# Gated linear attention before a ReLU-squared layer on one core: a chunk's first 32 keys join the state in one product, and every engine gets a written-out order

## The chip, the core and the metric

The kernel runs on one core of a Trainium2 chip. A core has a matrix engine (TensorE, PE in the profile; its weight loads are listed apart as PEld), three engines for elementwise work (VectorE or DVE, ScalarE or ACT, GpSimd or POOL), and a queue engine, SyncE or SP. SP, ACT and POOL also start DMA transfers. Each engine works through its own instructions in the order in which the program lists them, and waits on semaphores for the others. The metric is the device time of one execution in microseconds (us), the median of several runs; less is better. All inputs are float32.

## What is computed

For each of 4 x 8 (batch, head) pairs a complex decay runs over 768 steps of 48 features; its output feeds a two-layer block with a squared ReLU.

```python
mag = np.sqrt(a_re * a_re + a_im * a_im)
scale = np.minimum(mag, 0.999) / (mag + 1e-06)
a_re_n, a_im_n = (a_re * scale, a_im * scale)
for t in range(S):                       # S = 768, D = 48
    ar, ai = (a_re_n[:, :, t, :, None], a_im_n[:, :, t, :, None])
    new_re = ar * S_re - ai * S_im
    new_im = ar * S_im + ai * S_re
    kv = np.einsum('bhd,bhe->bhde', k[:, :, t], v[:, :, t])
    S_re, S_im = (new_re + kv, new_im)
    y[:, :, t] = np.einsum('bhd,bhde->bhe', q[:, :, t], S_re)
x = np.ascontiguousarray(y.transpose(0, 2, 1, 3)).reshape(B * S, H * D)   # 3072 x 384
h = x @ w_in                             # 384 x 2048
r = np.maximum(h, 0.0)
out = (r * r) @ w_out                    # 2048 x 384
```

## The kernel before

The 3072 rows are cut into 6 units of 512 steps (index `n`). In a unit the 8 heads form 4 pairs (index `i`, with `z = i // 2` for the half of the heads), and the 512 steps form 4 chunks of 128 (index `j`). For each unit the kernel works in these stages.

- `load` and `chain`: the inputs arrive in `aq` (gate, q, k) and `v`; DVE and ACT normalise the gates and multiply them up along the steps (a scan; its result is `xn`). `rest`/`apply` turn them into scaled queries and keys in `f`. Of the scaled keys, `gather` copies a version with the steps on the partitions into `KC`, by DMA.
- `turn` or `turn_pe`, once a pair: queries and keys are transposed into `QT`, with 96 rows (real and imaginary part of 48 features) and 128 columns for each chunk, head, and query or key. `turn_pe` does it on PE (line 1624) with ACT copies (line 1628), for the four pairs of unit 0 and three of unit 1; `turn` does it on DVE and with DMAs.
- `score(i, h)`, once a head: the 128 x 128 scores of each chunk, keys on the partitions of a PSUM bank (`sc`), steps on the columns (line 1645). A key acts only on later steps. So keys 0 to 63 are multiplied with all 128 steps and keys 64 to 127 with the last 64, in two products a chunk; each has 64 columns of weights, so one stands in PSUM partitions 0 to 63 and one in 64 to 127. In odd chunks the halves change places, so four successive products go to halves 0, 1, 1, 0. DVE then multiplies the bank with a mask (line 1648) into an `A` tile of 128 x 512.
- `keep(i)`: the state, 96 rows by 48 columns a head, grows by one chunk's keys times its `v` (line 1676, PSUM banks `tr`); sums go on DVE (line 1690), or on ACT where nothing came before (line 1686), into `St` and `S`.
- `mix(i)`: each chunk's output is `v` times the masked scores, 128 columns (line 1707), plus the state before the chunk times the queries, 128 columns (line 1711). The two heads of a pair write PSUM partitions 0 to 47 and 64 to 111. The state's product is left out where the sequence begins (chunk 0 of units 0 and 3, `fresh`) and where a new one begins inside a unit (chunk 2 of units 1 and 4, `cross`). ACT copies the result to `yt` (line 1720), a DMA brings it to `xT` (line 1733).
- `dense(n, grp)`: the first layer on `xT` (line 1758), squared ReLU on ACT (lines 1791 and 1792), then the second layer, as plain products (line 1806) or in `seven` by seven products of half size (line 1869) with sums on DVE (1885, 1894). `eleven` is the first layer of the last unit (line 2014). `rows` writes each 128 x 384 output tile with two DMAs on POOL's queue (line 1824).
- `convert` (lines 947 to 961): the weights arrive as raw 64-bit floats in tiles used for other things later (`KC`, `g`, `w`, `T`, `QT`, `xT`) and are turned into float32 by ACT and DVE; `fetch` (line 932) starts their DMAs on POOL's queue.

Nothing is issued at once. Every piece of work is a step with an engine, an estimated duration, keys that it reads and writes, and a rank; `Plan.order` runs them through a model of the engines' times, and `Plan.emit` issues them in the order of their modelled starts. Before, the engine takes the ready step of the lowest rank, and a table, `SHIFTS`, moves the ranks of some 200 steps by hand.

Of the kernel before, what the change touches and what calls it, by code (L numbers as in the profile page):

```python
# [16 lines left out]
ALU = mybir.AluOpType  # L17
# [464 lines left out]
class Plan:  # L482
# [3 lines left out]
    MARGIN = 0.3  # L486
    SLACK = 1.7
# [6 lines left out]
    SETTLED, GROUP = 90.0, 8  # L494
    HOLD, URGENT, FILL = {"DVE": 0.15, "ACT": 0.8}, (2, 0.2), (2, 0.2)
    DRAIN = {"DVE": 0.12, "ACT": 0.13}
    SHIFTS = {
        -1193.0: (320,),
        -802.0: (1256,),
        -595.0: (2284,),  # L500
        -594.0: (2285,),
        -500.0: (2041,),
        -301.0: (2694,),
        -210.0: (2688,),
        -108.0: (2690,),
        -100.0: (range(14, 17), 25, 37, 107, range(109, 111), 113, 166, 321, 344, 346, 356, 396,
            range(575, 577), 579, 625, range(1086, 1088), range(1245, 1247), 1271, 1304, 1306,
            1588, 1824, 1826, 2117, 2691, 2697, 2708, 2716,),
        100.0: (9, 11, range(20, 22), 24, 41, 104, 210, 234, 272, 279, 284, 304, 306, 314, 327,
            329, 331, 352, 354, 373, 375, 377, 379, 406, 408, range(410, 412), 417, 422, 424,  # L510
            range(431, 433), 440, range(443, 445), 448, range(452, 454), 466, 482, 496, 507, 564,
            range(681, 683), range(684, 686), 781, 783, 788, 800, 809, range(811, 814), 865, 869,
            885, 942, 1057, range(1116, 1118), 1123, 1129, 1132, 1146, 1164, range(1175, 1177),
            1188, range(1259, 1261), 1320, 1323, 1328, 1331, 1338, 1340, 1348, 1355, 1377, 1381,
            1384, 1389, 1392, 1406, 1478, 1480, 1729, 1737, 1740, 1748, 1763, 1781, 1792, 1794,
            range(1797, 1799), 1813, 1847, 1856, 1998, range(2043, 2045), 2071, 2073, 2135, 2147,
            2155, range(2163, 2165), 2180, range(2192, 2194), 2242, 2371, 2433,
            range(2445, 2447), range(2450, 2452), range(2456, 2458), 2459, 2472, 2474, 2545,
            2578, 2581, 2592, 2633,),
        189.0: (1283,),  # L520
        197.0: (2079,),
        200.0: (871,),
        292.0: (2097,),
        293.0: (2094,),
        302.0: (2233,),
        389.0: (2557,),
        503.0: (1815,),
        504.0: (1416,),
        588.0: (1405,),
        597.0: (1827,),  # L530
        602.0: (range(1665, 1668),),
        703.0: (1821,),
        793.0: (1345,),
        802.0: (2552,),
        805.0: (2616,),
        898.0: (779,),
        903.0: (378,),
        911.0: (441,),
        996.0: (2546,),
        1009.0: (1852,),  # L540
        1016.0: (831,),
        1209.0: (403, 425,),
        1516.0: (458,),
        1717.0: (484,),
        3014.0: (1380,),
        3126.0: (879,),
        3128.0: (419,),
        3315.0: (1166,),
        3422.0: (893,),
        3520.0: (1190,),  # L550
        4109.0: (27,),
        7784.0: (407,),
        9674.0: (414,),
        11185.0: (31,),
        11579.0: (35,),
        12886.0: (402,),
        12982.0: (39,),
# [30 lines left out]
    def order(self):  # L588
        steps = self.steps
        rank = [100.0 * s[4][0] + s[4][1] for s in steps]  # L590
        for shift, which in self.SHIFTS.items():
            for ns in which:
                for n in [ns] if isinstance(ns, int) else ns:
                    rank[n] += shift
        users = [[] for _ in steps]
        left = []
        for n, s in enumerate(steps):
            left.append(len(s[2]))
            for d in s[2]:
                users[d].append(n)  # L600
        engines = ("SP", "POOL", "PE", "DVE", "ACT")
        free = {e: 0.0 for e in engines}
        wait = {e: [] for e in engines}
        done, start, at = {}, {}, {}
        bus = warm = 0.0
        tiled = False

# [3 lines left out]
        def ready(n):  # L611
            e = steps[n][0]
            t = 0.0
            for d in steps[n][2]:
                same = steps[d][0] == e and steps[d][5] is None
                hop = self.HOP[steps[d][0]]
                if same:
                    hop = self.DRAIN.get(e, 0.0) if d in steps[n][7] else 0.0
                if e == "PE" and not same and done[d] > 100.0:
                    paired = steps[d][5] is not None and steps[n][6]  # L620
                    hop += self.SLACK if paired else self.MARGIN
                t = max(t, done[d] + hop)
            at[n] = t
            wait[e].append(n)

        for n in range(len(steps)):
            if not left[n]:
                ready(n)
        flown = {True: [], False: []}
        while len(start) < len(steps):  # L630
            best = None
            for e in engines:
# [66 lines left out]
def fast_path(ctx, tc, q, k, v, a_re, a_im, moe_w_in, moe_w_out, out, flag):  # L699
# [6 lines left out]
    C = 128  # L706
# [1470 lines left out]
```

## Time and profile before

| | us |
|---|---|
| median of 3 runs | 655.08 |
| the runs | 656.88, 655.08, 652.56 |
| the profiled execution, its time | 652.32 |
| the profiled execution, its span | 650.4 |

The profile is one execution. Its span runs from the first to the last instruction; the time of the same execution is 1.9 us more. Its granted TensorE clock was 0.991 of full speed in the mean. Line numbers such as L1645 are lines of the kernel before. A matmul of float32 stands in the trace as two records, each with its own weight load, so the 8 products of a score are 16 records. The profile gives for each engine its busy time, for each line its instructions, and for idle time what ended it. Neighbouring rows of the timeline overlap, because a product's record runs until its result is written; the pace is read from one start to the next.

### The profile page before, as it was taken

Reading aid. Unit: us, or ns where it says so; the run is one execution under the profiler, and the core shown is the slowest. Engines: PE = TensorE matmul, PEld = TensorE weight load, DVE = VectorE, ACT = ScalarE, POOL = GpSimd, SP = SyncE. Lnnn points to the kernel's source line nnn. Section 1 sums busy time; section 2 is a strip of 40 time slices with the busy share of each in tenths; the row PEclk is TensorE's granted clock in tenths of the full one; section 3 lists DMA queues with packets and bytes.
Section 4 is the critical chain, followed back from the end, with each engine's and each line's share of the span. In section 5 each row is a group of like instructions: output and inputs, shape, how many; then the busy total and the mean of one; then the engine's idle time right before and its main releaser. Section 6 shows DMA issues by size and latency. Waiting matters only on the chain.

```text
span 650.4 us, 12670 instructions
## 1 busy us (share of the span) xinstructions
PE 607.8 (93%) x4714; PEld 540.4 (83%) x4714; DVE 585.2 (90%) x1192; ACT 347.0 (53%) x635; POOL 122.0 (19%) x214
## 2 busy tenths in 40 slices
PE   0467999999999999999999999999999999999996
PEld 0356887688678988999989999989989989998996
DVE  7989999999998999998988999988998998459981
ACT  7479889888547244538353449354447442125500
POOL 7501140221100032040032030021040130051200
PEclk9979999999999999999999999999999999999999
DMA  6972787125620056452057580056370153377631
GB/s 210 298 268 50 162 220 202 42 50 147 174 53 1 1 126 163 127 156 41 7 144 176 128 182 2 13 138 177 101 183 0 26 132 92 82 240 270 213 116 30
DMA packets 55270, 80.39 MB, mean 124 GB/s; under 512 B 11392, under 2 KB 37920, under 8 KB 55200
## 3 DMA queue, kind: packets, MB, share of 16 engines
q0 software_dynamic: 15424, 42.12, 22.7%
q1 hardware_dynamic: 35168, 31.93, 19.3%
q10 hardware_dynamic: 4608, 5.44, 3.3%
q8 instruction: 39, 0.64, 0.4%
q14 instruction: 31, 0.25, 0.1%
HBM read 48.76 MB, written 4.72 MB: 82 GB/s over the span
## 4 chain that ended last, share of the span: by engine, by line
PE 72%; DVE 17%; DMA 5%; issue 2%; ACT 2%; POOL 0%; ACTq 0%; DVEq 0%; SPq 0%
PE d L1758 24%; PE d L1869 22%; PE d L1806 5%; PE sc L1645 4%; DVE f L1444 3%; PE yp L1707 3%; PE tr L1676 3%; PE yp L1711 2%; PE d L2014 2%; DMA w<-in_moe_w_in_dram 2%; PE tr L2014 2%; DVE g L1885 2%; DVE f L1509 2%; PE sc L2014 1%; DVE aq L1461 1%
## 5 line engine op out<-in xcount | busy, mean ns | idle before, releaser
L1758 PE MATMUL d<-xT,w 128*128 128x256 f32 x888 | 198.6, 380 | 1.5 <-DMA xT<-yt 1.2
L1758 PEld LDWEIGHTS d<-xT,w 128*128 128x128 f32 x888 | 167.3, 190 | 26.2 <-DMA xT<-yt 1.5
L1869 PE MATMUL d<-T,g 128*128 128x192 f32 x576 | 100.3, 329 | 0.3 <-DVE ot L1894 0.3
L1869 PEld LDWEIGHTS d<-T,g 128*128 128x128 f32 x576 | 93.6, 190 | 2.7 <-issue 1.1
L1791 ACT ACTIVATE g<-d 128x512 f32<-128x512 f32 x74 | 43.9, 593 | 69.9 <-PE d L1758 60.6
L1869 PE MATMUL d<-w,g 128*128 128x192 f32 x432 | 75.8, 328 | 0.0
L1869 PEld LDWEIGHTS d<-w,g 128*128 128x128 f32 x432 | 71.0, 190 | 1.2 <-ACT g L1791 0.2
L1824 POOL DMA_DIRECT2D out_dram<-ot x40 | 25.3, 638 | 218.4 <-DVE ot L1894 182.7
L1546 POOL DMA_DIRECT2D KC<-f x60 | 35.5, 600 | 112.2 <-DVE f L1509 82.6
L1885 DVE TENSOR_TENSOR g<-g 128x512 f32<-128x512 f32 x72 | 48.5, 684 | 7.6 <-ACT g L1792 4.4
L1792 ACT ACTIVATE g<-g 128x512 f32<-128x512 f32 x80 | 50.5, 631 | 2.5
L1444 DVE TENSOR_TENSOR f<-aq,xn 128x384 f32<-128x384 f32 (+1 forms) x72 | 46.8, 685 | 0.0
L1806 PE MATMUL d<-w,g 128*128 128x384 f32 x128 | 43.5, 489 | 0.2 <-DVE w L961 0.2
L1598 DVE STREAM_TRANSPOSE aq<-f 128x384 f32<-128x384 f32 (+1 forms) x51 | 42.2, 902 | 0.3
L1114 DVE TENSOR_TENSOR f<-aq 128x384 f32<-128x384 f32 x72 | 37.1, 552 | 0.5
L1645 PE MATMUL sc<-QT 96*64 96x64 f32 (+1 forms) x736 | 36.8, 249 | 0.5 <-ACT QT L1628 0.5
L1645 PEld LDWEIGHTS sc<-QT 96*64 96x64 f32 x736 | 34.2, 137 | 3.0 <-ACT QT L1628 1.2
L1806 PEld LDWEIGHTS d<-w,g 128*128 128x128 f32 x128 | 23.6, 190 | 15.4 <-DVE w L961 0.9
L1894 DVE TENSOR_TENSOR ot<-ot,d 128x192 f32<-128x192 f32 x70 | 23.3, 349 | 11.5 <-PE d L1869 11.2
L1475 ACT ACTIVATE f<-aq 128x768 f32<-128x768 f32 (+1 forms) x16 | 17.2, 1083 | 28.8 <-DVE aq L1461 28.7
L1037 POOL DMA_DIRECT2D v<-in_v_dram x30 | 23.2, 791 | 24.9 <-ACT f L1067 24.5
L1711 PE MATMUL yp<-QT,St 96*48 96x128 f32 x240 | 24.5, 272 | 0.0
(313 smaller groups left out, 1114.8 us busy)
## 6 DMA issues: line engine op xcount, KB each, us to landing
QT<-aq SPq DMA_DIRECT2D x136, 64.0 KB, 2.0
f<-in_moe_w_in_dram POOLq DMA_DIRECT2D x8, 768.0 KB, 8.1
f<-in_moe_w_out_dram POOLq DMA_DIRECT2D x8, 768.0 KB, 5.4
QT<-aq ACTq DMA_DIRECT2D x68, 64.0 KB, 2.3
KC<-f POOLq DMA_DIRECT2D x40, 96.0 KB, 3.4
out_dram<-ot POOLq DMA_DIRECT2D x40, 96.0 KB, 3.7
xT<-yt SPq DMA_DIRECT2D x34, 96.0 KB, 2.5
T<-in_moe_w_out_dram POOLq DMA_DIRECT2D x4, 768.0 KB, 11.0
```

The source lines that it names most:

```text
L1114: lambda c=c, j=j: dve.tensor_tensor(out=f[:, j], in0=a[:, :, :, c - 1], in1=a[:, j, :, c].unsqueeze(1).to_broadcast([C, 2, HH, D]), op=AL ...
L1444: lambda j=j, r=r: dve.tensor_tensor(out=f4[:, j, r], in0=a[:, r], in1=over(j), op=ALU.mult), rk)
L1546: lambda i=i, p0=p0, m=m, src=src, queue=queue: queue.dma_start(out=kc[p0:p0 + m, i], in_=src),
L1598: lambda src=src, dst=dst: dve.transpose(out=dst, in_=src), rank)
L1645: pe.matmul(sa[p0:p0 + CH, j, t0:], lhsT=T[:, j, 1, h, t0:t0 + CH], rhs=T[:, j, 0, h, t0:], start=True, stop=True)
L1711: pe.matmul(ps[64 * h:64 * h + D, j - js[0]], lhsT=at[j][:, h], rhs=T[:, j, 0, h], start=False, stop=True)
L1758: pe.matmul(ps, lhsT=w1[:, f // FP, m, ts(f % FP, C)], rhs=xT[:, n % 2, m, ts(grp, G)], start=(m == 0), stop=(m == NM - 1))
L1791: act.activation(out=o, in_=ps, func=AF.Relu)
L1792: act.activation(out=o, in_=o, func=AF.Square)
L1806: pe.matmul(ps, lhsT=gt[:, f % 2, ts(i, C)], rhs=w2[:, f], start=(f == 0), stop=(f == NF - 1))
L1869: pe.matmul(bank[b][:, 0:DH], lhsT=gsets[x][h][:, j - HW * h, r], rhs=w(j), start=first and j == 0, stop=last and j == NT - 1)
L1885: lambda: dve.tensor_tensor(out=g[:, :, o], in0=g[:, :, x0], in1=g[:, :, x1], op=op),
```

## The change

**The products.** A chunk's keys 0 to 31 act on its steps 0 to 31 in one block of 32 x 32 scores. Before, these scores are part of the `A` tile. Now DVE writes the masked block into rows 96 to 127 of the `QT` tile, below the 96 rows of the queries (`near`), and ACT copies `v`'s rows 0 to 31 into rows 96 to 127 of the state's tiles (`St`, `S`). One product of 128 rows then gives the state's part and this block's. The rest of the scores, steps 32 to 127, stays with `v` as a second product, of 96 columns. Both are now done for every chunk, so a state of zero is written by POOL where there was none. The rows under the queries of steps 32 to 127 must be zero: `clear` has POOL write them, again after the tiles have held raw weights.

A score now takes three products a chunk: keys 0 to 63 with steps 32 to 127 (96 columns, PSUM partitions 0 to 63); a 64-wide set of weights whose second half is keys 0 to 31, with steps 0 to 31 (32 columns, partitions 64 to 127); keys 64 to 127 with steps 64 to 127 (64 columns, partitions 64 to 127). The mask becomes two, for 384 columns and for 32 partitions by 128 columns.

**The layout.** In a chunk the steps are now grouped by 32 and not by 64, which needs four DMAs and not two for each output tile (`rows`). Odd chunks no longer change halves, so `v` and the gathered keys come in one DMA a chunk where odd chunks had two (`places`).

**The order.** `SHIFTS` and the choice by rank are gone. `ORDER` lists for each of the five engines the steps in the order in which it takes them (numbers count the engine's steps, sorted by rank). Steps of an engine start in that order and no other; the modelled times only interleave the engines.

```diff
-    SHIFTS = {
...
-        12982.0: (39,),
-    }
+    ORDER = {
+        "SP": """
...
+        "PE": """
+            539-554 0-1 555-559 2 560-561 3 562 4-7 563 8 564-567 42 568-571 45 572-573 43 574 44
...
+    }
     def places(i):
-        return [(CH, 0, CH), (0, CH, CH)] if i % 2 else [(0, 0, C)]
+        return [(0, 0, C)]
+
+    def clear(s, rank):
+        z = QT[s].rearrange("p (i h k x) -> p i h k x", i=W, h=2, k=2)[C - QC:C, :, :, 0]
+        keys = [("QT", s, 0), ("QT", s, 1)] + ([("t", 0), ("t", 1)] if s == 2 else [])
+        step("POOL", 0.9, [], keys, lambda: pool.memset(z, 0.0), rank)
...
             def go():
-                for j0 in range(0, W, 2):
-                    for half in range(2):
-                        for j in (j0, j0 + 1):
-                            p0, t0 = CH * (half ^ (j % 2)), CH * half
-                            pe.matmul(sa[p0:p0 + CH, j, t0:], lhsT=T[:, j, 1, h, t0:t0 + CH],
-                                      rhs=T[:, j, 0, h, t0:], start=True, stop=True)
+                for j in range(W):
+                    k0 = j * 4 * C + (2 * h + 1) * C
+                    for p0, at_, lo, hi in ((0, 0, QC, C), (CH, -QC, 0, QC), (CH, CH, CH, C)):
+                        pe.matmul(sa[p0:p0 + CH, j, lo:hi],
+                                  lhsT=QT[s][0:R, k0 + at_:k0 + at_ + CH],
+                                  rhs=T[:, j, 0, h, lo:hi], start=True, stop=True)
             step("PE", SCORE, [("QT", s, h)], [(b,)], go, rank, slack=True)
-            step("DVE", tt(L), [(b,)], AK[a], lambda: dve.tensor_tensor(
-                out=As[a].rearrange("p (j o t) -> p j o t", o=2, t=C),
-                in0=bank[b].rearrange("p (j o t) -> p j o t", o=2, t=C), in1=mask4,
-                op=ALU.mult), rank)
+            near = QT[s].rearrange("p (i h k t) -> p i k h t", i=W, k=2, h=2)[C - QC:C, :, 0, h, 0:QC]
+            step("DVE", tt(W * (C - QC)), [(b,)], AK[a], lambda: dve.tensor_tensor(
+                out=As[a][:, 0:W * (C - QC)].rearrange("p (j t) -> p j t", j=W),
+                in0=sa[:, :, QC:C], in1=far_mask, op=ALU.mult), rank)
+            step("DVE", tt(W * QC), [(b,)], [("q0", s, h)], lambda: dve.tensor_tensor(
+                out=near, in0=sa[C - QC:C, :, 0:QC], in1=near_mask, op=ALU.mult), rank)
...
+            step("ACT", ac(3 * 2 * D), [("v", vs(n))], [("sv", s)], lambda: act.copy(
+                out=sf[C - QC:C], in_=v5[0:QC, 1:W, 2 * i:2 * i + 2]), rank)
+            if cross:
+                step("POOL", 0.2, [], [("st", s, 2)], lambda: pool.memset(st[:, 1], 0.0), rank)
...
                         for h in range(2):
-                            pe.matmul(ps[64 * h:64 * h + D, j - js[0]], lhsT=v5[:, j, 2 * i + h],
-                                      rhs=aa[h][:, j], start=True, stop=at[j] is None)
+                            pe.matmul(ps[64 * h:64 * h + D, j - js[0]], lhsT=at[j][:, h],
+                                      rhs=T[:, j, 0, h], start=True, stop=False)
                         for h in range(2):
-                            if at[j] is not None:
-                                pe.matmul(ps[64 * h:64 * h + D, j - js[0]], lhsT=at[j][:, h],
-                                          rhs=T[:, j, 0, h], start=False, stop=True)
+                            pe.matmul(ps[64 * h:64 * h + D, j - js[0], QC:C],
+                                      lhsT=v5[:, j, 2 * i + h], rhs=aa[h][:, j],
+                                      start=False, stop=True)
...
+        if which[0] == 0:
+            Sn = Sb[n % 2]
+            if fresh:
+                step("POOL", 0.4, [], [("S", n % 2, i) for i in range(NP)],
+                     lambda: pool.memset(Sn[0:R], 0.0), (CHAIN, 0.3) if n == 0 else rank)
+            step("ACT", ac(DM), [("v", vs(n))], [("Sv", n % 2)], lambda: act.copy(
+                out=Sn[C - QC:C].rearrange("p (h d) -> p h d", h=H), in_=v5[0:QC, 0]), rank)
...
-        for p0 in (0, CH):
+        for p0 in range(0, C, QC):
             dma(pool, [("ot", o, 0), ("ot", o, 1)], [], lambda p0=p0: pool.dma_start(
-                out=out[r + p0:r + p0 + CH, :].rearrange("(t c) e -> c t e", c=W),
-                in_=ots[o][p0:p0 + CH]), (DENSE, n), CH * DM * 4)
+                out=out[r + p0:r + p0 + QC, :].rearrange("(t c) e -> c t e", c=W),
+                in_=ots[o][p0:p0 + QC]), (DENSE, n), QC * DM * 4)
```

In the rows below a name such as `sc_115` is a tile with its number, ahead of the arrow what is written, behind it what is read, then the shape that is written.

PE, unit 2 before: the end of a pair's two scores and what follows (L1645 is a score, L1869 the second layer, L1707 and L1711 the mix).

```order
L1645 MATMUL sc_115<-QT_75 64x128 x2
L1645 MATMUL sc_115<-QT_75 64x64 x2
L1645 MATMUL sc_115<-QT_75 64x128 x2
L1645 MATMUL sc_115<-QT_75 64x64 x2
L1645 MATMUL sc_116<-QT_75 64x128 x2
L1645 MATMUL sc_116<-QT_75 64x64 x2
L1645 MATMUL sc_116<-QT_75 64x128 x2
L1645 MATMUL sc_116<-QT_75 64x64 x2
L1869 MATMUL d_113<-w_67,g 128x192 x8
```

PE, unit 2 after: the end of a pair's scores, the first layer between, and the mix of the first chunks (L1674 is a score, L1805 the first layer, L1745 and L1748 the mix).

```order
L1674 MATMUL sc_116<-QT_74 64x96
L1674 MATMUL sc_116<-QT_74 64x32
L1674 MATMUL sc_116<-QT_74 64x64
L1805 MATMUL d_114<-xT,w_66 128x256 x3
L1805 MATMUL d_112<-xT,w_66 128x256 x6
L1805 MATMUL d_113<-xT,w_66 128x256 x6
L1745 MATMUL yp<-QT_74,S_88 48x128 x2
L1748 MATMUL yp<-xn,v_78 48x96
L1748 MATMUL yp<-e,v_78 48x96
L1745 MATMUL yp<-QT_74,St_92 48x128 x2
L1748 MATMUL yp<-xn,v_78 48x96
L1748 MATMUL yp<-e,v_78 48x96
```

A score goes from 8 products to 12, and every chunk's mix has four products, of 128, 128, 96 and 96 columns.

DVE before, the end of unit 0's attention: the masks of its last pair (L1648), state sums (L1690) and the conversion of weights around them (L954, L958, L961; L1070 is unit 1's chain).

```order
L954 TENSOR_SCALAR w_67<-w_67 128x768
L954 TENSOR_SCALAR w_67<-T 128x768
L961 ISA w_66<-xT,w_66 128x1536
L1648 TENSOR_TENSOR A_91<-sc_116,mask 128x512
L1070 TENSOR_TENSOR f_70<-f_70 128x768
L954 TENSOR_SCALAR w_66<-T 128x768
L1690 TENSOR_TENSOR St_93<-tr_118,St_93 96x96 x2
L961 ISA w_66<-T,w_66 128x1536
L954 TENSOR_SCALAR w_66<-g 128x768
L1648 TENSOR_TENSOR A_90<-sc_115,mask 128x512
L1648 TENSOR_TENSOR A_91<-sc_116,mask 128x512
```

DVE after, the same place (masks L1679 and L1682, state sums L1727, conversion L979, L983, L986).

```order
L1679 TENSOR_TENSOR A_91<-sc_116,mask 128x384
L983 SCALAR_TENSOR_TENSOR w_66<-g,w_66 128x768
L986 ISA w_66<-g,w_66 128x1536
L1727 TENSOR_TENSOR S_89<-tr_118,St_92 96x96
L986 ISA w_66<-w_67,w_66 128x1536 x2
L1679 TENSOR_TENSOR A_91<-sc_116,mask 128x384
L1682 TENSOR_TENSOR QT_75<-sc_116,mask 32x4x32
L1679 TENSOR_TENSOR A_90<-sc_115,mask 128x384
L1727 TENSOR_TENSOR St_93<-tr_118,St_93 96x96
L1682 TENSOR_TENSOR QT_75<-sc_115,mask 32x4x32
```

Other conversions than before stand ahead of the last masks, among them two of L958's kind (now L983) that came behind them.

POOL's queue at the start, before: the first transfers after the gates have arrived (L932 weights, L1021 q and k, L1037 v).

```order
L932 DMA KC_77<-in_moe_w_in_dram 128x3x512
L932 DMA g<-in_moe_w_in_dram 128x3x512
L1021 DMA aq_68<-in_q_dram 128x4x192
L1021 DMA aq_69<-in_q_dram 128x4x192
L1037 DMA v_78<-in_v_dram 64x8x48
L1037 DMA v_78<-in_v_dram 128x8x48
```

POOL's queue at the start, after (L957 weights, L1051 q and k).

```order
L957 DMA w_67<-in_moe_w_in_dram 128x3x512
L1051 DMA aq_68<-in_q_dram 128x4x192
L957 DMA w_67<-in_moe_w_in_dram 128x3x512
L1051 DMA aq_69<-in_k_dram 128x4x192
L1051 DMA aq_69<-in_q_dram 128x4x192
L957 DMA KC_77<-in_moe_w_in_dram 128x3x512
```

The weights for `KC_77`, first in the queue before, come seventh now, behind q and k and two other pieces of weights (k of `aq_68` stands ahead of these rows).

More of the change, by code (lines that the diff above doesn't have):

```diff
@@ L589, in order @@
         steps = self.steps
[L590 to L601, printed above, removed]
@@ L659, in order @@
+            sent = flown[e == "POOL"]
+            if steps[n][5] is not None and len(sent) >= self.LANES:
+                t = max(t, sent[-self.LANES] + self.LANDED)
+            return t
+        while len(start) < len(steps):
+            heads = [(ready(e), line[e][head[e]], e) for e in line if head[e] < len(line[e])]
+            t, n, e = min(h for h in heads if h[0] is not None)
+            head[e] += 1
             _, dur, _, _, _, wire, _, _ = steps[n]
@@ L804, in fast_path @@
     ypair = bank["yp"]
+    pool.memset(sums, 0.0)
     make_identity(nc, ident)
@@ L2085, in fast_path @@
         if n == 0:
+            for s in range(2):
+                clear(s, (CHAIN, 0.3))
+        if n == 0:
             for i in range(NPIECE):
```

318 lines of the change are left out of this document (175 added, 143 removed).

## Prediction

> **What bounds the kernel now.** I read the page first, then busy time by stage, the waits of PE, and PE's timeline.
>
> ```profile
> span 650.4 us, 12670 instructions
> ...
> PE 607.8 (93%) x4714; PEld 540.4 (83%) x4714; DVE 585.2 (90%) x1192; ACT 347.0 (53%) x635; POOL 122.0 (19%) x214
> ...
> PE 72%; DVE 17%; DMA 5%; issue 2%; ACT 2%; POOL 0%; ACTq 0%; DVEq 0%; SPq 0%
> ```
>
> PE and DVE are both nearly full, and the chain of work that ended last lies mostly on PE. A mean over the span doesn't say which one limits a stage, so I cut the span where PE's character changes. The columns are: stretch, length, busy time of PE, its weight loads, DVE, ACT, POOL, then granted clock and DMA.
>
> ```profile
> 0.00:20.00 20.00, 0.07 (x1) 0.08 (x1) 15.86 (x25) 14.65 (x27) 13.83 (x46) 1.00 0.75 219
> 20.00:42.50 22.50, 12.49 (x65) 11.74 (x65) 20.59 (x63) 12.32 (x26) 7.29 (x10) 0.77 1.02 342
> 42.50:84.40 41.90, 35.18 (x474) 28.80 (x474) 41.59 (x92) 36.82 (x68) 4.36 (x8) 1.00 0.44 104
> 84.40:640.00 555.60, 554.66 (x4144) 494.69 (x4145) 505.50 (x1010) 283.19 (x515) 96.53 (x151) 1.00 0.43 114
> 640.00:650.40 10.40, 5.39 (x34) 5.10 (x32) 1.69 (x5) 0.00 (x0) 0.00 (x0) 0.93 0.13 36
> ```
>
> There are two regimes. From 42.5 to 84.4 us DVE is busy 41.59 of 41.90 us: unit 0's attention hangs on DVE, and PE waits. From 84.4 to 640 us PE is busy 554.66 of 555.60 us, and DVE has 50 us to spare. From about 90 us on, PE's waits for others are these:
>
> ```profile
> PE d L1869 <- DVE ot L1894: 0.3, 1, 0.3
> PE tr L1676 <- DVE S L1690: 0.2, 1, 0.2
> PE d L1806 <- DVE w L961: 0.2, 1, 0.2
> ```
>
> So no order of steps can win anything there: the end is the moment at which PE becomes full, plus PE's work from then on, plus the tail. A change is worth what it adds to PE's work in units 1 to 5, and what it does to the 84.4 us.
>
> Busy time could hide idle time here, since records overlap. So I take the pace from starts, in unit 2 (start, length, engine, line, tiles and shapes, records).
>
> ```profile
> 240.92 4.15 PE L1758 MATMUL d<-xT,w 128*128 128x256 f32 x18
> 245.01 1.56 PE L1645 MATMUL sc<-QT 96*64 96x128 f32 x32
> 246.49 2.86 PE L1758 MATMUL d<-xT,w 128*128 128x256 f32 x12
> ...
> 255.27 0.84 PE L1676 MATMUL tr<-v,KC 128*64 128x48 f32 x23
> 255.89 0.32 PE L1645 MATMUL sc<-QT 96*64 96x128 f32 x1
> 255.94 0.22 PE L1676 MATMUL tr<-v,KC 128*64 128x48 f32 x1
> 256.00 1.52 PE L1645 MATMUL sc<-QT 96*64 96x128 f32 x31
> ...
> 264.15 0.43 PE L1707 MATMUL yp<-A,v 128*48 128x128 f32 x4
> 264.40 0.39 PE L1711 MATMUL yp<-QT,S 96*48 96x128 f32 x4
> 264.62 0.39 PE L1707 MATMUL yp<-A,v 128*48 128x128 f32 x4
> ...
> 265.94 0.26 PE L1676 MATMUL tr<-v,KC 128*64 128x48 f32 x4
> ```
>
> The first layer's 18 records of 256 columns take 4.09 us, 0.227 each, with no hole. In the mix four records of 128 columns (two heads, two records each) start every 0.22 us. The heads write different halves of the partitions and run side by side, so one half does a 128-column record in 0.11 us. A pair's two scores occupy PE from 245.01 to 246.49, 1.48 us.
>
> **The scores.** Before, each half of the array gets, for two chunks, two records of 128 columns and two of 64: 2 x 0.11 + 2 x 0.056 = 0.33 us. Two scores are four times that, 1.33, and 0.15 for starting and draining: the 1.48 measured. After, a chunk gives the lower half two records of 96 columns (0.165 us by the same rate) and the upper half two of 32 and two of 64. Counted in columns this is balanced, 96 and 96, and a score would cost what it did. But each of those records loads 64 columns of weights. What does a record cost whose weights are wider than its moving side? The state's products show it: 64 columns of weights, 48 moving. Twelve such records on one half (24 in all, the other half's have 33 columns) take from 255.27 to 256.00, 0.061 each with the first one's start, and not the 0.041 of 48 columns. A second place shows it more strongly, at a halved clock, in filling products with 128 columns of weights:
>
> ```profile
> 36.55 0.59 PE L1564 MATMUL d<-yt,ident 128*128 128x24 f32 x2 [8.49 <-DVE yt L1201]
> 36.97 4.60 PE L1564 MATMUL d<-ident 128*128 128x128 f32 x20
> 41.38 0.52 PE L1148 MATMUL tr<-ident,xn 128*128 128x128 f32 x3
> ```
>
> Two records with 24 moving columns take 0.42 us, 0.21 each; twenty with 128 take 4.41, 0.22 each. The narrow ones gain nothing. So a record of 32 columns behind 64 columns of weights should cost what one of 64 does, 0.057. The upper half then needs 4 x 0.057 = 0.228 us a chunk, and sets the pace; two scores take 8 x 0.228 + 0.15 = 1.97 us. That is 0.49 more a pair. Units 1 to 5 have 20 pairs: **+9.7 us**. The bounds: no more than the columns (0.165 a chunk), +0; or each start waiting for the one ahead of it in program order, which I price below at +13.4. I stay near 9.7 because the state's products are the nearest row.
>
> **The mix.** Before, a chunk with a state takes 2 x 0.22, a pair 1.76 us (264.15 to 265.94 is 1.79). After it takes 0.22 + 0.165 a chunk, 1.54 a pair. But the pairs of units 1, 3 and 4 skipped one chunk's state product, 7 x 0.22 = 1.54, and now do it. Only the 8 pairs of units 2 and 5 gain: **-1.8 us**. In units 0, 1, 3 and 4, two thirds of the pairs, the joint product gains nothing.
>
> **The start.** Until 84.4 us DVE decides, so I count its rows from the first use of `xn` to unit 0's last mask.
>
> ```profile
> L1648 DVE TENSOR_TENSOR A<-sc,mask 128x512 f32<-128x512 f32 x28 | 18.3, 681 | 1.9 <-PE sc L1645 1.9
> L1690 DVE TENSOR_TENSOR St<-tr,St 96x96 f32<-96x96 f32 x32 | 7.7, 248 | 0.9 <-PE yp L1711 0.4
> ...
> L954 DVE TENSOR_SCALAR w<-T 128x768 uint32<-128x768 uint32 x5 | 2.8, 553 | 0.0
> ...
> L961 DVE CUSTOM_DVE_ANT_0 w<-g,w 128x1536 uint16<-128x1536 uint16 x2 | 1.9, 962 | 0.1
> L958 DVE SCALAR_TENSOR_TENSOR w<-g,w 128x768 uint32<-128x768 uint32 x2 | 1.9, 953 | 0.0
> ```
>
> ```profile
> L1509 DVE TENSOR_TENSOR f<-f,aq 128x384 f32<-128x384 f32 x20 | 10.5, 550 | 0.1
> ```
>
> Ahead of the last mask stood 6 conversions of L954's kind and 3 of L961's, 6 x 0.55 + 3 x 0.96 = 6.2 us. Now it is 5, 4, and 2 of L958's kind: 2.75 + 3.84 + 1.91 = 8.5. Each of the 8 masks becomes one over 384 columns (0.55, as L1509) and one over 32 partitions, which no row shows: I take the state sum's 0.25 (96 x 96), between nothing and that; together 0.12 more than 0.68, in all +1.0. One state sum fewer: -0.25. The sum is +3.0, or about +2.5 by starts, since neighbouring records overlap by 0.08. Against it stand two idle times of DVE in the scan, and the row of the first full work of PE:
>
> ```profile
> 34.11 0.43 DVE L1197 TENSOR_TENSOR KC<-yt 128x96 f32<-128x96 f32 x2 [0.83 <-ACT yt L1222]
> ...
> 35.89 0.30 DVE L1197 TENSOR_TENSOR KC<-yt 128x36 f32<-128x36 f32 x2 [0.34 <-ACT yt L1222]
> ```
>
> ```profile
> 80.06 1.28 DVE L1648 TENSOR_TENSOR A<-sc,mask 128x512 f32<-128x512 f32 x2
> ```
>
> ```profile
> 84.38 1.53 PE L1758 MATMUL d<-xT,w 128*128 128x256 f32 x6 [1.25 <-DMA xT<-yt]
> ```
>
> ACT's copies of L1222 came behind weight conversions; in the new order they stand ahead of them, so 1.2 us can go. The last masks (80.06) release the last mix, its copy, its DMA, and PE's first layer at 84.38. I take 2.5 - 1.2 = **+1.3 us**, with -2 to +4 as its range. Unit 0's eight longer scores lie under DVE's work.
>
> **What I cost at nothing.** On DVE 40 masks of 0.12 more, 5 us, under the 50 idle us of the full stretch. On ACT 30 copies of `v`, 0.25 to 0.5 each, some 10 us, where 283 of 555 are used. POOL gets 40 more output issues and 15 memsets, and loses 24 gather and `v` issues; SP loses 12.
>
> ```profile
> L1824 POOL DMA_DIRECT2D out_dram<-ot x40 | 25.3, 638 | 218.4 <-DVE ot L1894 182.7 <-ACT ot L1811 25.2 <-DVE f L1114 7.6
> ```
>
> An output tile now needs four issues of 0.64 us, so its buffer comes free 1.3 us later, and DVE's sums into the next one are queued behind that wait; POOL waits 218 us at this line, so there is room. If these covers fail, the price is a PE wait of a microsecond or two at a unit's seam. At the start the conversion of the `KC` weights stands in ACT's queue ahead of the scan's copies:
>
> ```profile
> 27.77 0.48 ACT L1163 COPY e<-tr 128x384 f32<-128x384 f32 x1
> ```
>
> ```profile
> KC<-in_moe_w_in_dram POOLq DMA_DIRECT2D x1, 768.0 KB, 5.0
> ```
>
> That transfer landed 5.0 us after its issue when it was first. Now 3.1 MB go ahead of it; at the 342 GB/s of the second stretch that is 9 us more, about 23 us on the clock. The scan's copies run at 27.8, so some 4 us cover it.
>
> **The sum.** 652.3 + 9.7 - 1.8 + 1.3 = 661.5 us for the profiled execution. That execution lies 2.8 us under the median of 655.1, so I add the same 9.2 to the median: **664 us**, 1.4% slower. About 1%, 6.5 us, is what a measurement of this kernel can tell from no change.
>
> **The rivals.**
>
> *Weight loads hide, not slower.* If a 32-column record costs its 32 columns, 0.028 us, half against half stays balanced and the scores cost nothing: 655.1 - 1.8 + 1.3 = 655. The place is the upper half in L1674; there are 40 scores x 8 such records. The change turns from within 1% to slower when the record costs more than about 0.05 us (320 records x 0.022 = 7). For it speaks that the two halves load their weights apart; against it speak the 24-column rows. Chance 0.12.
>
> *Starts in program order.* If no product may start ahead of one that precedes it, a chunk costs 0.08 (the second 96-column start) + 3 x 0.057 = 0.25 us, a score 1.0 against 0.67, and 40 scores +13.4: 668. The rows at 255.89 and 255.94 speak against it: a score's record starts before the last record of the state's products, which precede it in the program. Chance 0.08. The Trainium skill, "TensorE: Matmul & The Clock Gate", Part 3, The mechanism, states this rule (strict FIFO for starts, no reordering); the trace disagrees at those two rows.
>
> *New waits.* The order has no choice at run time: one late transfer (the `KC` weights, `v` behind the weights, the zeroed rows on POOL) holds an engine and all behind it. At 5 us or more it gives 669 to 675. Against it: the 4 us of cover. Chance 0.07.
>
> *The order wins at the start.* Slower scores and all, faster by over 1% needs some 16 us out of the first 84; DVE's idle time there is 8.5 us, mostly before the gates arrive. Chance 0.06, with 640 to 648.
>
> **How the numbers follow.** My forecast has 0.67. About a fifth of it stays under 6.5 us (0.14, same), the rest is slower (0.53). With the second and third rival slower is 0.66; same is 0.14 and 0.11 from the first rival, 0.25; faster is 0.06 and small parts of the rest, 0.09. The range, 654 to 672, leaves out the fourth rival, half of the first, and the worst of the third: 2 in 10.
>
> **What would show it.** Two scores between other work should take 1.9 to 2.0 us from start to start where 1.48 stood; 1.5 would refute the largest term. The mix of a pair in units 2 and 5 should take 1.54. PE should stay full after its first long run of first-layer work, and that run should begin at 84 to 88 us. A PE wait of several microseconds after 90 us would show a cover that failed; PE's first long run before 80 us would prove me wrong about the order.

## The result, and the profile after

The changed kernel took 663.89 us (median of 4 executions, 663.46 to 665.14) where the kernel before took 654.99: a ratio of 1.0141, with a 95% interval of 1.0105 to 1.0177. 664 was predicted. In the experiments below 14 of 64 executions (those with 32 columns of weights apart) took 8 to 11 us longer than the others of their kernel; the medians leave these out, and so do the ratios, except that of the run without the near product, which holds two.

The page of the changed kernel, its span, busy times and the chain that ended last:

```profile
span 662.1 us, 13619 instructions
...
PE 617.8 (93%) x5162; PEld 550.5 (83%) x5162; DVE 594.5 (90%) x1240; ACT 359.0 (54%) x665; POOL 139.8 (21%) x243
...
PE 84%; DVE 10%; ACT 2%; DMA 2%; issue 1%; ACTq 0%; DVEq 0%; SPq 0%
```

Busy time by stage (the same columns as before), and all waits of PE for others between 88 and 655 us:

```profile
42.50:84.40 41.90, 37.27 (x530) 30.69 (x530) 40.86 (x92) 38.79 (x72) 5.76 (x9) 0.96 0.37 89
84.40:651.50 567.10, 565.42 (x4560) 506.20 (x4560) 515.62 (x1058) 299.13 (x550) 112.96 (x181) 1.00 0.42 112
651.50:662.10 10.60, 3.24 (x20) 2.95 (x19) 1.24 (x4) 0.00 (x0) 0.00 (x0) 0.76 0.15 45
```

```profile
PE d L1916 <- DVE g L1932: 0.7, 1, 0.7
PE d L1805 <- ACT g L1838: 0.5, 1, 0.5
PE sc L1674 <- issue: 0.3, 1, 0.3
```

The picture is that of before, made longer: PE is full from 84 us on, DVE has some 51 us to spare there, and no wait over 0.7 us stands on PE. In PE's timeline, at a place in unit 2, stand the mix of a pair and behind it two scores:

```profile
256.25 0.43 PE L1745 MATMUL yp<-QT,S 128*48 128x128 f32 x4
...
257.82 2.04 PE L1674 MATMUL sc<-QT 96*64 96x96 f32 x48
259.79 4.17 PE L1916 MATMUL d<-w,g 128*128 128x192 f32 x24
```

The scores take from 257.82 to 259.79, 1.97 us, where 1.48 stood; that is the predicted number. The mix takes 1.57, from 256.25 to 257.82 (1.79 before, 1.54 predicted).

For the whole kernel I gave each record of PE the time from its start to the next record's start, with idle holes apart, and added up by kind of step from the end of unit 0's last mix. "Start" is the moment at which that mix ended, less 0.217 us for each record of the first layer that PE had done by then (2 before, 6 after), and those records are counted with the first layer. "Before again" is a second profiled execution of the kernel before. The last two columns are experiments that leave out part of the work: the near product, which is that of a chunk's keys 0 to 31 with its steps 0 to 31, and most of the mask that follows it.

| us | before | before again | after | no near product | and small near mask |
|---|---|---|---|---|---|
| start | 83.9 | 84.9 | 86.3 | 85.8 | 85.6 |
| scores | 29.7 | 29.7 | 38.1 | 27.9 | 27.7 |
| state products | 14.9 | 14.9 | 15.7 | 16.3 | 16.4 |
| mixes | 34.0 | 34.0 | 31.7 | 33.2 | 32.5 |
| first layer | 209.7 | 210.2 | 209.0 | 209.3 | 209.2 |
| second layer and the rest | 272.3 | 272.2 | 272.5 | 273.7 | 273.2 |
| PE idle | 0.9 | 1.7 | 1.5 | 4.3 | 2.2 |
| tail behind PE's last product | 5.0 | 5.5 | 7.4 | 5.6 | 5.5 |
| span | 650.4 | 652.9 | 662.1 | 656.1 | 652.4 |

From "before again" to "after" that is 8.4 for the scores, 0.9 for the state products (which partly run beside the scores), -2.3 for the mixes, +1.4 at the start, -1.2 in the first layer and +1.9 in the tail, 9.2 us with the small rows, as the spans give (652.9 and 662.1). The first profile's execution was 2.5 us shorter, so against it the span rose by 11.7. The tail was not in my sum. Its rows, before and then after (PE's last products, DVE's last sums into the output tiles, the output transfers):

```profile
642.63 2.76 PE L1869 MATMUL d<-T,aq 128*128 128x192 f32 x16
642.83 0.35 DVE L1894 TENSOR_TENSOR ot<-ot,d 128x192 f32<-128x192 f32 x1 [1.59 <-PE d L1869]
643.21 0.33 SPq L1818 DMA_DIRECT2D out_dram<-ot  x1
645.43 0.35 DVE L1894 TENSOR_TENSOR ot<-ot,d 128x192 f32<-128x192 f32 x1 [2.25 <-PE d L1869]
645.82 0.38 ACTq L1818 DMA_DIRECT2D out_dram<-ot  x1
```

```profile
653.28 1.46 PE L1916 MATMUL d<-T,aq 128*128 128x192 f32 x8
654.78 1.27 DVE L1941 TENSOR_TENSOR ot<-ot,d 128x192 f32<-128x192 f32 x4 [6.14 <-PE d L1916]
655.16 2.09 SPq L1865 DMA_DIRECT2D out_dram<-ot  x3
656.09 0.41 ACTq L1865 DMA_DIRECT2D out_dram<-ot  x1
```

Before, one sum and one transfer were left when PE ended. After, four sums wait 6.14 us for PE and then four transfers go out. PE's last steps stand in another order: the product that the first of the four sums needs comes last, and the other three queue behind it on DVE.

### The profile page after: what moved, and what is told of

The parts are those of the page before. It is cut to its first block, busy times and chain, and to the rows that moved or that the text cites. A ratio compares the mean times of both kernels' runs of the same rounds, so it can differ in the third digit from the quotient of the medians.

```text
span 662.1 us, 13619 instructions
## 1 busy us (share of the span) xinstructions
PE 617.8 (93%) x5162; PEld 550.5 (83%) x5162; DVE 594.5 (90%) x1240; ACT 359.0 (54%) x665; POOL 139.8 (21%) x243
## 4 chain that ended last, share of the span: by engine, by line
PE 84%; DVE 10%; ACT 2%; DMA 2%; issue 1%; ACTq 0%; DVEq 0%; SPq 0%
PE d L1916 27%; PE d L1805 27%; PE d L1853 6%; PE sc L1674 6%; PE yp L1745 3%; PE tr L1713 2%; PE yp L1748 2%; PE d L2061 2%; PE tr L2061 2%; PE sc L1805 2%; PE sc L2061 1%; DVE f L1474 1%; PE tr L1654 1%; PE yp L2061 1%; PE yp L1805 1%
## 5 line engine op out<-in xcount | busy, mean ns | idle before, releaser
L1805 PE MATMUL d<-xT,w 128*128 128x256 f32 x888 | 198.1, 380 | 0.5 <-ACT g L1838 0.5
L1805 PEld LDWEIGHTS d<-xT,w 128*128 128x128 f32 x888 | 167.5, 190 | 25.1 <-ACT g L1838 0.9
L1871 POOL DMA_DIRECT2D out_dram<-ot x80 | 48.3, 608 | 137.5 <-DVE ot L1941 115.7
L1576 POOL DMA_DIRECT2D KC<-f x48 | 31.0, 652 | 201.1 <-DVE f L1539 93.3
L1674 PE MATMUL sc<-QT 96*64 96x96 f32 (+2 forms) x1104 | 49.3, 235 | 0.3 <-issue 0.3
L1674 PEld LDWEIGHTS sc<-QT 96*64 96x64 f32 x1104 | 46.2, 137 | 2.5 <-issue 2.1
L1628 DVE STREAM_TRANSPOSE aq<-f 128x384 f32<-128x384 f32 (+1 forms) x51 | 43.6, 908 | 0.3
L1941 DVE TENSOR_TENSOR ot<-ot,d 128x192 f32<-128x192 f32 x70 | 23.4, 348 | 14.9 <-PE d L1916 14.5
L1745 PE MATMUL yp<-QT,St 128*48 128x128 f32 x268 | 27.0, 273 | 0.0
L1759 ACT COPY yt<-yp 112x512 f32<-112x512 f32 (+1 forms) x20 | 11.6, 578 | 26.2 <-PE yp L1748 24.8
```

Of the source, the lines that this page charges most:

```text
L1628: lambda src=src, dst=dst: dve.transpose(out=dst, in_=src), rank)
L1674: pe.matmul(sa[p0:p0 + CH, j, lo:hi], lhsT=QT[s][0:R, k0 + at_:k0 + at_ + CH], rhs=T[:, j, 0, h, lo:hi], start=True, stop=True)
L1745: pe.matmul(ps[64 * h:64 * h + D, j - js[0]], lhsT=at[j][:, h], rhs=T[:, j, 0, h], start=True, stop=False)
L1805: pe.matmul(ps, lhsT=w1[:, f // FP, m, ts(f % FP, C)], rhs=xT[:, n % 2, m, ts(grp, G)], start=(m == 0), stop=(m == NM - 1))
L1871: dma(pool, [("ot", o, 0), ("ot", o, 1)], [], lambda p0=p0: pool.dma_start(out=out[r + p0:r + p0 + QC, :].rearrange("(t c) e -> c t e", c= ...
```

## The experiments

**The kernel before, once more.** No edit.

> The kernel before, run and profiled once more, to see where its executions differ. The profiled one took 652.3 us, 2.7 under the median of the runs. If the difference is in the tail (from the start of the last product's end at 645.4 to the end of the span, 5.0 us there), the 7.7 us tail of the changed kernel is partly chance; I expect the tail within 0.5 us of 5.0, and the 2 to 4 us more of a usual execution ahead of 84 us, in the transfers and in PE's clock there.

654.89 us, span 652.9. Start +0.9 against the first profile, idle +0.8, tail 5.5, first layer +0.5; the scores and mixes are the same to 0.1. So executions differ by a microsecond at the start and by half a one in the tail, and the 7.4 of the changed kernel is outside that.

**Narrower weights: 32 columns.**

```diff
-for p0, at_, lo, hi in ((0, 0, QC, C), (CH, -QC, 0, QC), (CH, CH, CH, C)):
-    pe.matmul(sa[p0:p0 + CH, j, lo:hi], lhsT=QT[s][0:R, k0 + at_:k0 + at_ + CH],
+for p0, m, at_, lo, hi in ((0, CH, 0, QC, C), (C - QC, QC, 0, 0, QC), (CH, CH, CH, CH, C)):
+    pe.matmul(sa[p0:p0 + m, j, lo:hi], lhsT=QT[s][0:R, k0 + at_:k0 + at_ + m],
```

> The product of a chunk's first 32 keys loads 32 columns of weights (the 32 keys alone, written to the last 32 partitions) where it loaded 64. Theory (a record costs the wider of its two sides): the upper half then needs 2 x 0.028 + 2 x 0.057 = 0.17 us a chunk, about the lower half's 0.165, two scores take 1.5 us where 1.97 stood, 20 pairs give 9.4 us back: 654.5 us (653 to 657). Rival, a fixed price of 0.057 for any short record: two scores stay at 1.97, 664. Rival, starts in program order: 0.194 a chunk, 1.70 for two scores, 658.5.

719.8 us for the profiled execution (six lie between 719.8 and 745.4), ratio on record 1.1111 (1.1063 to 1.1158): worse than every theory. Two scores, between a mix and the second layer:

```profile
276.12 4.23 PE L1675 MATMUL sc<-QT 96*64 96x96 f32 x48
280.28 0.92 PE L1917 MATMUL d<-w,g 128*128 128x192 f32 x4
```

4.16 us, 0.52 a chunk. The records of 32 columns of weights carry the tile 96*32 in the trace, those around them 96*64, and the array changes tile size twice a chunk. The Trainium skill, "TensorEngine Tiling (Array Packing)", Key Properties, says that a change of the tiling mode drains the array. The trace agrees so far: (4.16 - 1.97) / 8 = 0.27 us a chunk for two changes. The run said nothing on what weights cost, since it changed a second thing that I had not thought of.

**Wider moving side.** `(CH, -QC, 0, QC)` becomes `(CH, -QC, 0, CH)`.

> The same product with 64 moving columns (steps 0 to 63) behind its 64 columns of weights where it had 32; the 32 added columns lie where the mask is zero or the third product writes over them. Theory (the wider side counts): free, two scores stay at 1.97 us and the time at 664 (663 to 666). Rival, a record costs its moving columns and something fixed on top: 16 records of a score pair's upper half with 32 more columns, 16 x 0.027 = 0.43 us a pair, 672.5 us.

664.7 us, ratio 1.0145 (1.0123 to 1.0168). Two scores:

```profile
258.05 2.04 PE L1674 MATMUL sc<-QT 96*64 96x96 f32 x48
260.02 0.59 PE L1916 MATMUL d<-w,g 128*128 128x192 f32 x2
```

1.97 again. Twice the moving columns behind the same weights are free, so the columns are not what the near product costs.

**The tail's order.** In PE's list `530-531 533-535 537-538 536 532` becomes `530-538`.

> PE's last eight steps (the halves of the last output tiles' second layer) stand in the order in which they stood in the kernel before; all else is that of the changed kernel. In the changed kernel four sums of DVE and four output transfers come behind PE's last product, before one sum and one transfer. Theory: the tail from PE's last product to the end of the span goes from 7.7 us back to about 5.0 to 5.6, and the time to 661.5 (661 to 662.5). Rival: a transfer's own time sets the tail, and it stays within 0.5 us of 7.7, 664.

662.4 us, ratio 1.0118 (1.0101 to 1.0135). Its profile, with a span of 670.6 us, holds the event that the last section shows; its tail is as before the change:

```profile
661.94 2.76 PE L1916 MATMUL d<-T,aq 128*128 128x192 f32 x16
...
664.74 0.35 DVE L1941 TENSOR_TENSOR ot<-ot,d 128x192 f32<-128x192 f32 x1 [2.25 <-PE d L1916]
665.12 0.38 ACTq L1865 DMA_DIRECT2D out_dram<-ot  x1
```

One sum and one transfer at the end, 5.9 us behind PE where 7.4 stood, and 1.5 us of the time, the smaller end of what I expected.

**Narrower weights without a change of tile: 33 columns.**

```diff
-for p0, at_, lo, hi in ((0, 0, QC, C), (CH, -QC, 0, QC), (CH, CH, CH, C)):
+for p0, m, at_, lo, hi in ((0, CH, 0, QC, C), (CH, QC + 1, 0, 0, QC), (CH, CH, CH, CH, C)):
...
-in0=sa[C - QC:C, :, 0:QC], in1=near_mask
+in0=sa[CH:CH + QC, :, 0:QC], in1=near_mask
```

> As the run with 32 columns of weights, but with 33 (32 keys and the one behind them), so that the product keeps a tile of 64 columns, as the state's products with 33 columns do; it is written to partitions 64 to 96, and the near mask reads partitions 64 to 95 there and writes to 96 to 127 as ever. Theory (a record costs the wider of its sides, and what the 32-column tile cost was the change between tile sizes, (4.16 - 1.97) / 8 = 0.27 us a chunk): no change of tile size, upper half 2 x 0.03 + 2 x 0.058 = 0.176 us a chunk, two scores 1.5 to 1.6 us where 1.97 stood; 20 pairs give 8 to 9.4 us back, and up to 2 more in unit 0, where PE is full from 70 us on: 653.5 us (652.5 to 656). Rival, a fixed price of 0.058 for any short record: 1.97 for two scores, 664. Rival, any change of weights' width within a half drains it: about 4.1 for two scores, 720.

663.0 us, ratio 1.0128 (1.0099 to 1.0156). And together with the tail's order:

> The 33 columns of weights and the last eight steps of PE in the order of the kernel before, both together. If the two are independent, 1.5 us less than with the 33 columns alone: 652 us by the theory, 662.5 by the rival of a fixed price per record.

659.7 us, ratio 1.0082 (1.0052 to 1.0113). That is 3.3 us below the 33 columns alone, where 1.5 was expected; in the two profiles the tail is 8.2 and 6.0 us, which shows 2.2 of it, and the rest is open. In the second run two scores take

```profile
551.02 1.81 PE L1675 MATMUL sc<-QT 96*64 96x96 f32 x48
552.77 0.43 PE L1917 MATMUL d<-w,g 128*128 128x192 f32 x1
```

1.75 us: neither my 1.5 to 1.6 nor the rival's 1.97. Weights' width counts, but half as much as I had said. The records' own starts on the upper half, from 551.24 us on, suggest the reason: within a chunk they are 28, 33, 86 and 58 ns apart, the sum 0.205 us. In the changed kernel's profile, with 64 columns of weights throughout, the same four are 31, 58, 86 and 58, the sum 0.233, which is four times 58. A stream of 64 columns takes about 55 ns, by the lower half's records of 96 columns, which start every 82. So the mended rule is that a load is hidden behind the *preceding* record's stream: one step costs the greater of this record's moving columns and the next record's weight columns. After the second short stream a load of 58 sticks out. The rule is read from the sums; the single starts don't show it step by step (33 and 86 stand where it has 58 and 58).

**The order within a score.** The near products of the four chunks stand together:

```diff
+for j, part in ((0, 0), (0, 1), (1, 1), (2, 1), (1, 0), (3, 1),
+                (0, 2), (2, 0), (1, 2), (2, 2), (3, 0), (3, 2)):   # part 0: lower, 1: near, 2: upper
```

> The run with 33 columns of weights and the old tail, and the 12 products of a score in another order: the four near products stand together, then the upper half's four others. With 33 columns two scores took 1.74 us, not the 1.5 to 1.6 that I had expected; the starts on the upper half are 28, 33, 86, 58 ns apart, 0.205 us a chunk. Theory, mended: a record's stream hides the next record's weight load, so that the step from one record to the next costs the greater of the one's moving columns and the other's weight columns. After a near record (28 ns of stream) a load of 64 columns (58 ns) sticks out, once a chunk, which gives 28 + 58 + 58 + 58 = 0.202. Grouped, it sticks out once a score: 7 x 28 + 9 x 58 = 0.718 us a score, 1.44 + 0.15 = 1.59 us for two, 3 us less over 20 pairs: 657 us (656 to 658). Rival, a load of 33 columns has a price of its own of 44 ns wherever it stands: 8 x 44 + 8 x 58 = 0.816 a score, 1.74 for two as before, 660.

> The same order of products, but with 64 columns of weights for the near product, as in the changed kernel (old tail too). Every load takes 58 ns and no stream is longer, so by the mended theory the order changes nothing: 16 x 58 = 0.93 us a score, 1.97 for two, 662.4 us, the time of the run with the old tail alone. If the grouping itself wins (less of the start and drain, or a better fit of the two halves), this run shows it: 1.8 or less, 659.

With 33 columns 659.0 us, ratio 1.0062 (1.004 to 1.0083); with 64 columns 662.2, ratio 1.0107 (1.0073 to 1.0142). First 33 (in a profile with a span of 668.1 that holds the last section's event, ahead of these rows), then 64:

```profile
561.36 1.67 PE L1676 MATMUL sc<-QT 96*64 96x96 f32 x48
562.96 0.43 PE L1918 MATMUL d<-w,g 128*128 128x192 f32 x1
```

```profile
258.43 2.04 PE L1676 MATMUL sc<-QT 96*64 96x96 f32 x48
260.40 0.43 PE L1918 MATMUL d<-w,g 128*128 128x192 f32 x1
```

1.60 against 1.59 expected, and 1.97 against 1.97: the mended rule holds, and a price of its own for each narrow load does not. That 1.59 came so close is partly luck. On the upper half the second score starts 0.752 us after the first, not 0.718: the narrow records follow each other every 33 ns, not 28, so there the load of 33 columns sets the step (7 x 33 + 9 x 58 = 753). What two scores take beyond that is 0.10 us, not 0.15. The time fell by 0.7 us (1.3 by the ratios, whose intervals overlap), not by the 3 that 20 pairs give. Something gives the rest back.

**What gives it back.** The near product is dropped from the changed kernel's list, with the old tail: `((0, 0, QC, C), (CH, CH, CH, C))`.

> The changed kernel with the old tail, the product of a chunk's first 32 keys and steps left out (its mask still runs, on what stands in the bank). The lower half's two records of 96 columns then set the pace, 0.165 us a chunk: two scores take 1.48 us, and the time falls by the whole price of that product, 20 x 0.49 = 9.8 us by the prediction, 662.4 - 9.8 = 652.6 us. Unit 0's scores, if they count too, would take off up to 2 us more: 650.6.

657.8 us, where 652.6 was expected (ratio 1.008, 1.0044 to 1.0116). By the table the scores fell by 10.2 us, as they should. But PE's idle time rose by 2.8, its mixes by 1.5, the second layer and the rest by 1.2. PE's waits from 88 us on:

```profile
PE d L1916 <- DVE g L1932: 1.4, 1, 1.4
PE yp L1745 <- DVE QT L1682: 0.8, 3, 0.3
PE d L1805 <- ACT g L1838: 0.6, 1, 0.6
PE tr L1654 <- ACT T L1658: 0.4, 1, 0.4
PE yp L1748 <- DVE xn L1679: 0.3, 1, 0.3
PE sc L1674 <- issue: 0.2, 1, 0.2
```

The mix (L1745, L1748) now waits for both masks (L1682 near, L1679 far). To see whether the masks are the cause, the near mask was cut to a quarter, `near[:, 0:1]` for `near`, once with the near product and once without:

> The changed kernel with the old tail, and the near mask of each score made over one chunk's row instead of four (32 x 32 elements for 32 x 128: the rest is left out). DVE saves some 0.1 us 48 times, 5 us. Theory: with scores at 1.97 us DVE keeps its cover, so PE is not served sooner, and the time stays at 662.4 (661.5 to 663). Rival: the masks are late in the changed kernel already, and 1 to 3 us come back: 660.

> The same small mask, in the kernel without the near product, which took 657.7 us where I had expected 652.6: its scores gave back the 10.2 us, but PE's idle time rose by 2.9 us, its mixes by 1.6 and its second layer and sums by 1.2. Theory: with cheap scores PE runs ahead of DVE's masks (two instructions a score now), and waits; with 5 us less of DVE's work 1.5 to 3 us come back: 655 to 656. Rival: what PE waits for is the written order itself or transfers, not DVE's masks: 657.5.

With the near product 661.5 us, ratio 1.0121 (1.0093 to 1.0148), against 1.0118: 0.9 us less by the medians, none by the ratios, no difference that can be told. Without it 654.3, ratio 0.9994 (0.9978 to 1.001): 3.5 us less than with the whole mask, a little more than expected. PE's waits for the masks are gone there:

```profile
PE d L1916 <- DVE g L1932: 1.2, 1, 1.2
PE d L1805 <- ACT g L1838: 0.5, 1, 0.5
PE tr L1654 <- ACT T L1658: 0.4, 1, 0.4
```

So the same 5 us of DVE's work cost a microsecond at most behind slow scores, and 3.5 us behind fast ones. That is not all that was given back: with the small mask in both, leaving out the near product gains 7.2 us (661.5 to 654.3), still 3 short of 10.2. By the table (the last column against "after") the 3 lie in the state products, the mixes, the second layer and PE's idle time, 0.7 to 0.8 each; no run separates them.

**The start.** In the grouped kernel two conversions of weights (573 and 571 in DVE's list) were moved behind unit 0's last masks.

> The grouped order with 33 columns (659 us), and at the start two conversions of weights moved behind unit 0's last masks on DVE, 1.8 us of work. There the last scores end at 83.2 us and their masks begin at 83.8, behind those conversions. Theory (the conversions ahead of the last masks set the start): the last mix begins 0.6 us earlier, PE's steady run at 85.9 instead of 86.5 (counted with the six products it has done by then), the time 658.4. Rival: the first layer then waits for the converted weights and it is 659 or more.

659.6 us, ratio 1.0074 (1.0054 to 1.0093): no gain. The rows show what came instead (DVE, then PE):

```profile
85.76 1.83 DVE L986 CUSTOM_DVE_ANT_0 w<-w,w 128x1536 uint16<-128x1536 uint16 x2
...
88.07 0.25 DVE L1729 TENSOR_TENSOR St<-tr,St 96x96 f32<-96x96 f32 x1
```

```profile
88.38 0.42 PE L1747 MATMUL tr<-QT,St 128*48 128x128 f32 x4 [0.94 <-DVE St L1729]
```

Three of the last four masks came 0.8 us earlier; the fourth, behind another state sum, came when it had. The conversions now stand ahead of the last state sum, and the last mix waits 0.94 us for it. Nor did the masks hold up this mix before the move: in the grouped kernel's profile PE waits for a transfer of keys, works on without a hole, and begins the mix at 86.16, when the last mask has been done for 0.45 us.

```profile
83.87 0.87 PE L1715 MATMUL tr<-v,KC 128*64 128x48 f32 x24 [0.69 <-DMA KC<-f]
```

Whether the start could be shorter with the state sum moved too was not tried.

No version that computes the whole result is faster than the kernel before: the best, grouped with 33 columns and the old tail, is 0.6% slower.

## Why the prediction was right

**The scores**, the largest term, were right in size (1.97 us a pair as predicted; in all 8.4 us, and 0.9 in the state products beside them, for 9.7). The step that gave it, that a record of 32 columns behind 64 columns of weights costs what one of 64 does, is shown by the run with 64 moving columns. The rule I drew behind it, that a record costs the wider of its own two sides, is not: it gave 1.5 to 1.6 for 33 columns and 1.75 was measured. All weights in the changed score have 64 columns, and there the two rules give the same number. Part of the exactness is luck: 8 x 0.233 + 0.10 was measured, 8 x 0.228 + 0.15 predicted.

**The mixes**: -2.3 for -1.8. Units 2 and 5 give 2.1 of it, as predicted, and the rate is right (1.57 a pair for 1.54).

**The start**: +1.4 to +2.3 for +1.3, by the one or the other profile of before. DVE's two waits for ACT in the scan went, as predicted. The near mask took 0.30 us a score, where I had put 0.25. That the last masks alone set the start isn't shown: in the changed kernel PE waits 0.21 us for the last one, but the last state sum comes next, and with faster scores a transfer of keys stands ahead of both, as the rows of the last experiment show.

**The tail**: +1.9 to +2.4, where my sum had nothing. I compared the orders at the start and at the unit's seams and never at the end, though the tail is the one other place besides the start where nothing hides a step. The order of PE's last steps accounts for 1.5 us of it. This miss is made up for by the first layer (0.7 to 1.2 us less, by a cause that is open), by the scores' 0.5 and by the mixes' 0.5. So each large term was right, but that the whole came within 0.1 us is luck.

**DVE's masks at nothing**: right for this kernel, as the small mask shows. But the reason I gave, 50 idle us in the full stretch, doesn't carry that far: the cover is where the mix comes after its scores, not in the stretch's sum. With scores faster by 10 us, 3.5 us of masks come to light. So the change's second price lay hidden under its first, and taking the near product away gives back 4.6 us of its 10.2.

**The rivals.** That weight loads hide is refuted by 1.97, and by the 33 columns that made two scores faster with the moving side unchanged. Starts in program order would have given 2 x 1.0 + 0.15 = 2.15 for two scores. The Trainium skill states that order ("TensorE: Matmul & The Clock Gate", Part 3, The mechanism); the trace, with 1.97, doesn't show it between the two halves of the partitions. New waits did not come in the changed kernel's profile: the longest wait of PE behind 88 us is 0.7. But in three profiles of its variants PE waits 7.1 to 7.3 us near 112 us, since weights stand behind one copy in POOL's queue (last section), which is the kind of wait that this rival named. Those kernels differ from the changed one by a few products or by the tail, so that none of its four executions met this may be luck. The start did not win.

## What to carry to other kernels

Count a small product by what follows it: its moving columns have to hide the next product's weight load, so halving the moving side of a product behind full weights gains nothing, and narrow products belong next to each other. Keep all products of one stretch in one tile size. When a saving on the busiest engine brings half of what it should, list that engine's waits anew: what was hidden at its old pace may not be at the new one; and wherever an order is written anew, compare its last steps too, since nothing comes after them to hide what they leave.

## What I had not expected of the hardware

A change of the tile's column size between 32 and 64 cost 0.27 us for a change and the change back (0.30 when counted from the 1.75 us of the 33 columns), though both products lie in the upper half and the lower half's tile stayed the same; with 33 columns, which keep the larger tile, there was none. The two runs also write the product to different partitions, 96 to 127 and 64 to 96, and no run separates that from the size.

In the profile of the run with the tail's order, a copy of one column on POOL took 13.2 us, where it takes 0.5 in the profile of the changed kernel:

```profile
90.75 13.22 POOL L2157 COPY gate<-xT 128x1 f32<-128x1 f32 x1 [16.67 <-DMA xT<-yt]
...
102.17 1.74 DVE L1124 TENSOR_TENSOR aq<-aq,f 128x1536 f32<-128x1536 f32 x1
103.91 1.43 POOL L957 DMA_DIRECT2D QT<-in_moe_w_out_dram  x2
108.79 0.88 ACT L972 ACTIVATE QT<-QT 128x768 uint32<-128x768 uint32 x1 [8.47 <-DMA QT<-in_moe_w_out_dram]
```

The copy ended when DVE's row at 102.17 did, at 103.9, and DVE then stood still, since ACT in its turn waited for the weights behind that copy in POOL's queue. PE lost 7.3 us by it at 111.9. The profiles of the runs with 33 columns of weights, alone and grouped with the old tail, have the same copy at the same place with 13.2 and 12.9 us, and PE's wait of 7.3 and 7.1 behind it; no other profile has it. The Trainium skill, "SBUF — State Buffer", Who interferes with whom, states that DVE and GpSimd share a pair of ports, and that a DVE instruction which needs that pair and a GpSimd one keep each other out for a whole instruction. The trace is in keeping with a lock, but a lock of one instruction doesn't give 13 us: 17 rows of DVE ran while the copy lasted, and in the changed kernel's profile the same 17 ran within 0.1 us of the same times, and the copy took 0.48 us. No run here took the copy or DVE's work away, so the cause isn't shown.
